# Fused HGRN2 attention and square-plus MLP: four output buffers, a last eviction in two column halves, one eviction placed earlier

## The chip, the cores and the metric

The kernel runs on one core of a Trainium2 chip. The time is that of one execution on the device, in microseconds, and the lower the better. The kernel before takes 192.82 us, the median of five runs (192.39 to 195.28). The profile is that of one further execution.

Five engines work side by side, each through its own list of instructions in order: TensorE (PE, matrix products into PSUM), VectorE (DVE), ScalarE (ACT), GpSimd (POOL) and SyncE (SP), which here only starts DMA transfers. ScalarE and GpSimd start some transfers too. An instruction that waits for a semaphore holds up everything behind it on its engine.

## What is computed

A gated linear recurrence over 768 steps for 4 x 8 heads of size 48, then a two-layer MLP on all 3072 tokens:

```python
f = 1.0 / (1.0 + np.exp(-f_logit))
for t in range(S):
    state = f[:, :, t, :, None] * state + np.einsum('bhd,bhe->bhde', k[:, :, t], v[:, :, t])
    y[:, :, t] = np.einsum('bhd,bhde->bhe', q[:, :, t], state)
...
x = attn_out.transpose(0, 2, 1, 3).reshape(B * S, H * D)    # 3072 x 384
h = x @ w_in                                                # 3072 x 2048
g = 0.5 * (h + np.sqrt(h * h + 4.0))
out = g @ w_out                                             # 3072 x 384
```

## The kernel before

The tokens are cut into 12 pairs of two blocks, 256 tokens a pair (p = 0 to 11), 128 a block. Each pair goes through the recurrence in its chunked form (small matrix products, line 424 to line 511) and then through the MLP. What follows is the MLP part, since the change touches its end alone.

- `m1.p.m` (line 551, m = 0 to 7): six matmuls that make 256 columns of h for the pair, in one PSUM bank.
- `sq.p.m` (line 560) and `rt.p.r` (line 566) on ScalarE: the square, and the square root for two m at once. `gt.p.m` (line 576) on VectorE: 0.5 h + r into the tile `g`.
- `m2.p.cn` (line 588): four matmuls each. For block c of the pair (c = 0 or 1) n runs from 0 to 3; after n = 3 one PSUM bank holds 128 tokens x 384 columns of the output. So `m2.10.03` is the last of pair 10's block 0.
- `ev.p.c` (line 595): the eviction, a copy of that bank into half c of the pair's tile `os` (128 x 2 x 384, fp32, line 597), on ScalarE (the copy of line 138) or VectorE (line 140). Tiles of the name `os` go round through `DEPTH['os']` buffers (line 29), by p modulo the depth. A copy into a buffer waits until the stores that read it before have landed.
- `st.p.cs.i` (line 605): a store to memory. i picks the partitions 0 to 63 or 64 to 127. For pairs 0 to 10 a store takes both blocks (`st10.01.0` and `st10.01.1`, 192 KB each), so it needs both evictions. For pair 11 each block has its own two stores, 96 KB each (`SPLIT_OUT`, line 26).

There is no scheduler at run time or build time: the string `ORDER` (lines 32 to 106) lists all pieces by name, with the engine behind the colon (S SyncE, A ScalarE, D VectorE, P GpSimd, T TensorE) and the PSUM banks behind the @. Lines 695 to 703 emit the pieces in this order, so it is each engine's program order. The waits are put in by the framework from what each instruction reads and writes. The list ends so:

```
gt11.2:D m2.10.03:T m1.11.4:T@4 gt11.3:D m2.11.10:T@2 sq11.4:A m2.11.00:T@0 ev9.1:A rt11.2:A m2.11.11:T st9.01.1:S st8.01.1:S
m2.10.12:T gt11.5:D st9.01.0:S m2.11.01:T gt11.4:D m2.10.13:T m2.11.02:T ev10.1:A m2.11.03:T ev10.0:A st10.01.0:S m2.11.12:T
ev11.0:D st10.01.1:S m2.11.13:T st11.0.0:A st11.0.1:S ev11.1:A st11.1.1:A st11.1.0:S
```

Read for ScalarE alone the end is: `ev9.1`, `rt11.2`, `ev10.1`, `ev10.0`, issue of `st11.0.0`, `ev11.1`, issue of `st11.1.1`. For SyncE: `st9.01.1`, `st8.01.1`, `st9.01.0`, `st10.01.0`, `st10.01.1`, `st11.0.1`, `st11.1.0`. VectorE ends with `gt11.5`, `gt11.4`, `ev11.0`.

Of the kernel before, what the change touches and what calls it, by code (L numbers as in the profile page):

```python
# [8 lines left out]
FP32 = mybir.dt.float32  # L9
FP16 = mybir.dt.float16  # L10
# [15 lines left out]
SPLIT_OUT = [11]  # L26
NHL = 2
NQK = 3
DEPTH = {'f': 3, 'q': 3, 'k': 3, 'v': 3, 'UT': 3, 's': 2, 'ep': 2, 'ea': 2, 'v16': 4, 'ge': 3, 'gs': 4, 'gb': 3, 'qkT0': 2, 'qkT1': 2, 'pm00': 2, 'pm01': 2, 'pm10': 2, 'pm11': 2, 'st0': 1, 'pc': 4, 'st1': 1, 'sn0': 2, 'sn1': 2, 'y16': 2, 'xT': 5, 'hsq': 3, 'r16': 3, 'g': 4, 'os': 2}
VDMA = []  # L30

ORDER = """
lf0.0:S lf0.1:S lq0.0:S lk0.0:S lq0.1:S TABLE:e ex0.0:A lf1.0:S ut0.0:D ex0.1:A tt0.0:D lk0.1:S ut0.1:D hi0.0:A ln0.0:A
# [66 lines left out]
m1.11.7:T@4 gt9.7:D st8.01.0:S m1.11.6:T@6 rt10.2:A m1.11.0:T@5 sq11.1:A gt10.4:D m2.9.03:T sq11.0:A m2.10.00:T@7 ev9.0:D  # L100
rt11.0:A m1.11.3:T@0 gt10.5:D m2.9.10:T@3 sq11.6:A gt11.1:D m2.10.10:T@1 sq11.3:A gt11.0:D m2.9.11:T sq11.7:A m1.11.2:T@2
m1.11.5:T@5 sq11.2:A m2.10.01:T sq11.5:A m2.10.02:T rt11.3:A m2.10.11:T rt11.1:A gt11.6:D m2.9.12:T gt11.7:D m2.9.13:T
gt11.2:D m2.10.03:T m1.11.4:T@4 gt11.3:D m2.11.10:T@2 sq11.4:A m2.11.00:T@0 ev9.1:A rt11.2:A m2.11.11:T st9.01.1:S st8.01.1:S
m2.10.12:T gt11.5:D st9.01.0:S m2.11.01:T gt11.4:D m2.10.13:T m2.11.02:T ev10.1:A m2.11.03:T ev10.0:A st10.01.0:S m2.11.12:T
ev11.0:D st10.01.1:S m2.11.13:T st11.0.0:A st11.0.1:S ev11.1:A st11.1.1:A st11.1.0:S
"""

ENGINES = {"D": "vector", "P": "gpsimd", "A": "scalar", "S": "sync", "T": "tensor"}
# [19 lines left out]
def describe(nc, W, ctx_tiles, aps):  # L128
    q, k, v, f_logit, moe_w_in, moe_w_out, out = aps
    T, sb, ps, K = ctx_tiles  # L130
    NP, H, D, NJ, NN, DM = 12, 8, 48, 3, 16, 384
# [4 lines left out]
    def copy(e, o, i):  # L136
        if e == "A":
            nc.scalar.copy(out=o, in_=i)  # L138
        else:
            eng(e).tensor_copy(out=o, in_=i)  # L140
# [3 lines left out]

    src = {"f": f_logit, "q": q, "k": k, "v": v}

    for i in range(4):
        def win(e, b, i=i):
            nc.gpsimd.dma_start(out=K["win"][i], in_=moe_w_in[:, i * 512:(i + 1) * 512].rearrange("(j p) n -> p j n", p=128))
        W.add(f"wi{i}", "P", win, makes=[f"win{i}"], dma=("w", 2.37), cost={"P": 0.83})  # L150

    for i in range(4):
        def wout(e, b, i=i):
# [3 lines left out]
    for p in range(NP):  # L157
        parts = [(0, 4), (4, 8)] if p in FINE else [(0, 8)]
        xs = range(len(parts))
        n = 384 // len(parts)  # L160
        b, c0 = divmod(p * 2, 6)
# [5 lines left out]
        for x, (h0, h1) in enumerate(parts):  # L167
            hs = slice(h0, h1)
            nh = h1 - h0
            for s in ("fqk" if p in VDMA else "fqkv"):  # L170
                def load(e, bk, s=s, x=x, hs=hs, p=p):
                    if (s, p) not in T:
# [5 lines left out]
                      dma=("l", 1.55 * nh / 8), cost={"S": 0.6})  # L178

            def ex(e, bk, x=x, hs=hs, p=p):  # L180
# [3 lines left out]
                  cost={"A": 0.2 + 0.84e-3 * 2 * n})  # L184

            last = x == len(parts) - 1
            if p in SPLIT:
                def ln(e, bk, x=x, hs=hs, p=p):
                    nc.scalar.activation(out=K["l32"][:, :, hs, 0:D], in_=T["f", p][:, hs].rearrange("p h i d -> p i h d"), func=AF.Ln, bias=1.0)
                W.add(f"ln{p}.{x}", "A", ln, reads=[f"e{p}.{x}"], makes=[f"s{p}.{x}"], uses=[("f", p), ("l32", p)], table="e",  # L190
                      cost={"A": 0.2 + 0.85e-3 * 2 * n})

                def cu(e, bk, x=x, hs=hs, h0=h0, h1=h1, p=p, last=last):
# [8 lines left out]
                    if last:  # L202
# [5 lines left out]
                      uses=[("l32", p)], banks=[f"cx{p}", f"c1{p}"], mode="F", cost={"T": 2.8 * nh / 8 + (1.0 if last else 0.0)})  # L208

                for i in range(2):  # L210
                    for nm, sgn, slot in (("ea", -1.0, 2 * i), ("ep", 1.0, 1 + 2 * i)):
                        def xp(e, bk, i=i, sgn=sgn, slot=slot, hs=hs, h0=h0, h1=h1, p=p):
                            if ("UT", p) not in T:
# [4 lines left out]
                              uses=[("UT", p), ("bank", f"c{'x1'[i]}{p}")], table="e", cost={"A": 0.17 + 0.85e-3 * n})  # L218

                for s, nm, en in ((0, "q", "ea"), (1, "k", "ep")):  # L220
                    for i in range(2):
                        def qm(e, bk, s=s, i=i, nm=nm, hs=hs, h0=h0, h1=h1, p=p):
# [3 lines left out]
                              uses=[(nm, p), ("UT", p), ("qk", p)], lock=True, cost={"D": 0.14 + 1.1e-3 * n, "P": 0.1 + 2.3e-3 * n})  # L226

            else:
# [14 lines left out]
                def ln(e, bk, x=x, hs=hs, p=p):  # L243
# [3 lines left out]
                    if ("s", p) not in T:  # L247
# [3 lines left out]
                      cost={"A": 0.2 + 0.85e-3 * n})  # L251

                if p not in DIRECT:
                    direct = p in HI_ACT

                    def hi(e, bk, x=x, hs=hs, p=p, direct=direct):
# [3 lines left out]
                        else:  # L260
                            copy(e, o, T["s", p][:, hs])
                    W.add(f"hi{p}.{x}", "A" if direct else "DPA", hi, reads=[f"t{p}.{x}" if direct else f"s{p}.{x}"], makes=[f"hi{p}.{x}"],
                          uses=[("UT" if direct else "s", p), ("hl", p)], table="e" if direct else None, lock=True, cost={"D": 0.07 + 0.9e-3 * n, "P": 0.19 + 0.86e-3 * n, "A": 0.2 + 0.85e-3 * n})
# [9 lines left out]
                def cu(e, bk, x=x, hs=hs, h0=h0, h1=h1, p=p, last=last, mats=mats):  # L273
# [12 lines left out]
                    if last:  # L286
# [10 lines left out]
                      cost={"T": full * len(mats) / 2 * nh / 8 + ((0.24 if p not in DIRECT else 0.5) if last else 0.0)})  # L297

                if p in ADD1:
                    def c1(e, bk, x=x, hs=hs, h0=h0, h1=h1, p=p):  # L300
                        if ("ea", p) not in T:
# [4 lines left out]
                          uses=[("ea", p), ("s", p), ("bank", f"cx{p}")], cost={"D": 0.15 + 1.05e-3 * n})  # L306

                for m, nm, sgn in ((0, "ep", 1.0), (1, "ea", -1.0)):
# [5 lines left out]
                    if m == 1 and p in ADD1:  # L314
                        W.add(f"{nm}{p}.{x}", "A", xp, reads=[f"cumi{p}.{x}"], makes=[f"{nm}{p}.{x}"], uses=[(nm, p)], table="e",
                              cost={"A": 0.2 + 0.85e-3 * n})
                    else:
                        W.add(f"{nm}{p}.{x}", "A", xp, reads=[f"cum{p}.{x}"], makes=[f"{nm}{p}.{x}"],
                              uses=[(nm, p), ("bank", f"c{'x1'[m]}{p}")], table="e", cost={"A": 0.17 + 0.85e-3 * n})
# [13 lines left out]
                for s, nm, en in ((0, "q", "ea"), (1, "k", "ep")):  # L333
                    def qm(e, bk, s=s, nm=nm, en=en, x=x, hs=hs, h0=h0, h1=h1, p=p):
                        for i in range(2):
# [3 lines left out]
                          uses=[(nm, p), (en, p), ("qk", p)], lock=True, cost={"D": 0.18 + 1.15e-3 * 2 * n, "P": 0.2 + 2.3e-3 * 2 * n})  # L339
# [20 lines left out]
        def ge(e, bk, p=p):  # L360
# [3 lines left out]
              cost={"A": 0.18})  # L364
# [14 lines left out]
        for cc in range(2):  # L379
            if p in XBAR:  # L380
                def tx(e, bk, cc=cc, p=p):
# [4 lines left out]
                      dma=("x", 1.9), cost={"S": 1.25})  # L386
        if p not in XBAR:
            for x, (h0, h1) in enumerate(parts):
# [15 lines left out]
                for cc in range(2):  # L404
                    def te(e, bk, x=x, j0=j0, j1=j1, cc=cc, p=p):
                        if ("qkT", p, cc) not in T:
# [3 lines left out]
                    m = (j1 - j0) * 256  # L410
                    W.add(f"te{p}.{cc}.{x}", "DA", te, reads=[f"tr{p}.{x}"], makes=[f"qkT{p}.{cc}"],
                          uses=[(f"qkT{cc}", p), ("bank", f"t{'AB'[cc]}{p}")], cost={"D": 0.15 + 0.53e-3 * m, "A": 0.17 + 0.83e-3 * m})

        both = [f"qkT{p}.0", f"qkT{p}.1"]
        for i in range(2):
# [12 lines left out]
            for h in range(2):  # L428
                key = f"{p}.{i}{h}"
                if key in PMACT:  # L430
                    def pc(e, bk, i=i, h=h, p=p):
# [3 lines left out]
                          cost={"A": 0.6})  # L435

                def pm(e, bk, i=i, h=h, p=p, key=key):
# [4 lines left out]
                      uses=[(f"pm{i}{h}", p), ("pc", 4 * p + 2 * i + h) if key in PMACT else ("bank", f"s{i}{h}.{p}")],  # L442
# [101 lines left out]
                      cost={"D": 0.35, "A": 0.49})  # L544

        for m in range(8):
            def m1(e, bk, m=m, p=p):
                T["h", p, m] = ps(bk[0], [128, 2, 2, 128], FP32)
                for a in range(2):
                    for j in range(NJ):  # L550
                        nc.tensor.matmul(out=T["h", p, m][:, a], lhsT=K["win"][m // 2][:, j, m % 2 * 256 + a * 128:m % 2 * 256 + a * 128 + 128],  # L551
                                         rhs=T["xT", p][:, :, j, :], start=(j == 0), stop=(j == NJ - 1))
            W.add(f"m1.{p}.{m}", "T", m1, reads=[f"xT{p}", f"win{m // 2}"], makes=[f"h{p}.{m}"], uses=[("xT", p)],
                  banks=[f"h{m}.{p}"], mode="F", cost={"T": 0.665})
            r, a = divmod(m, 2)

            def sq(e, bk, m=m, r=r, a=a, p=p):
                if ("hsq", p, r) not in T:
                    T["hsq", p, r] = sb("hsq", 4 * p + r, [128, 2, 512], FP16)
                nc.scalar.activation(out=T["hsq", p, r][:, a], in_=T["h", p, m].rearrange("p a c t -> p (a c t)"), func=AF.Square, scale=1.0)  # L560
            W.add(f"sq{p}.{m}", "A", sq, reads=[f"h{p}.{m}"], makes=[f"hsq{p}.{r}"], uses=[("bank", f"h{m}.{p}"), ("hsq", 4 * p + r)],
                  cost={"A": 0.585})
            if a == 1:
                def rt(e, bk, r=r, p=p):
                    T["r16", p, r] = sb("r16", 4 * p + r, [128, 2, 512], FP16)
                    nc.scalar.activation(out=T["r16", p, r], in_=T["hsq", p, r], func=AF.Sqrt, scale=0.25, bias=1.0)  # L566
                W.add(f"rt{p}.{r}", "A", rt, reads=[f"hsq{p}.{r}"], makes=[f"r16{p}.{r}"], uses=[("hsq", 4 * p + r), ("r16", 4 * p + r)],
                      table="s", cost={"A": 1.065})
# [13 lines left out]
        for cc in range(2):  # L582
            for n4 in range(4):
                def m2(e, bk, cc=cc, n4=n4, p=p):
                    if n4 == 0:
                        T["o", p, cc] = ps(bk[0], [128, DM], FP32)
                    for jn in range(4 * n4, 4 * n4 + 4):
                        nc.tensor.matmul(out=T["o", p, cc], lhsT=T["g", p][:, jn, cc * 128:(cc + 1) * 128],  # L588
                                         rhs=K["wout"][jn // 4][:, jn % 4, :], start=(jn == 0), stop=(jn == NN - 1))
                W.add(f"m2.{p}.{cc}{n4}", "T", m2,  # L590
                      reads=[f"g{p}.{2 * n4}", f"g{p}.{2 * n4 + 1}", f"wout{n4}"] + ([f"o{p}.{cc}{n4 - 1}"] if n4 else []),
                      makes=[f"o{p}.{cc}{n4}"], uses=[("g", p)] + ([("bank", f"o{cc}.{p}")] if n4 else []),
                      banks=[f"o{cc}.{p}"] if n4 == 0 else [], mode="F", cost={"T": 0.66})

            def ev(e, bk, cc=cc, p=p):
                if ("os", p) not in T:
                    T["os", p] = sb("os", p, [128, 2, DM], FP32)
                copy(e, T["os", p][:, cc], T["o", p, cc])
            W.add(f"ev{p}.{cc}", "DA", ev, reads=[f"o{p}.{cc}3"], makes=[f"os{p}.{cc}"], uses=[("bank", f"o{cc}.{p}"), ("os", p)],
                  cost={"D": 0.56, "A": 0.48})  # L600

        split = [[0], [1]] if p in SPLIT_OUT else [[0, 1]]
        for cs in split:
            for i in range(2):
                def st(e, bk, cs=cs, i=i, p=p):
                    c, n = cs[0], len(cs)
                    t0 = p * 256 + c * 128
                    eng(e).dma_start(out=out[t0:t0 + 128 * n, :].rearrange("(c u i) d -> i u c d", c=n, i=2)[i],
                                     in_=T["os", p][64 * i:64 * i + 64, c:c + n])
                W.add(f"st{p}.{''.join(map(str, cs))}.{i}", "SPA" if p in SPLIT_OUT else "S", st, reads=[f"os{p}.{c}" for c in cs], makes=[],  # L610
                      uses=[("os", p)], dma=("o", 0.28 * len(cs)), cost={"S": 0.6, "P": 0.8, "A": 0.6})


# [1 line left out]
def kernel(  # L615
# [10 lines left out]
    nc = tc.nc  # L626
# [53 lines left out]
        nc.gpsimd.tensor_copy(out=mask[:, i].rearrange("p (i t) -> p i t", i=2), in_=tri2[:, 1].unsqueeze(1).broadcast_to([128, 2, 64]))  # L680
    nc.gpsimd.tensor_copy(out=mask[:, 1, 0:64], in_=tri2[:, 0])

    win = [konst.tile([128, 3, 512], FP16, name=f"win{i}") for i in range(4)]
    wout = [konst.tile([128, 4, 384], FP16, name=f"wout{i}") for i in range(4)]

    def sb(name, seq, shape, dt):
        return sbp.tile(shape, dt, name=name, tag=f"{name}_{seq % DEPTH[name]}", bufs=1)

# [45 lines left out]
```

## Time and profile before

| | |
|---|---|
| median of five runs | 192.82 us |
| the profiled execution, whole | 192.7 us |
| its span, first to last instruction | 190.7 us |
| TensorE busy | 171.6 us, 90% |
| ScalarE busy | 156.9 us, 82% |
| VectorE busy | 150.4 us, 79% |
| GpSimd busy | 111.7 us, 59% |
| copies of `os` on ScalarE | 13, 478 ns each |
| copies of `os` on VectorE | 11, 551 ns each |
| stores of `os` issued by SyncE, by ScalarE | 24, 2 |
| last matmul ends | 185.2 us |
| granted TensorE clock, mean | 0.976 |

The profiled execution is one of its own, 0.1 us under the median of the five. Its span leaves out 2.0 us that lie around the first and the last instruction. A share of busy time is a mean over the whole span: here TensorE is at nine tenths or more in nearly every slice from 68 us to 185 us, and idle or waiting for data in much of the first 68 us. What an edit at the end of the kernel is worth is read from the last few microseconds, and from the question whether anything before them waits for what it touches. All times below are us from the start of the span.

### The profile page before, as it was taken

The page shows a single profiled execution, that of the slowest core. Times are in us where ns is not written, and L with a number is a line of the kernel's source. Part 1 is how long each engine was busy: PE and PEld are TensorE (multiplying, and loading weights), DVE is VectorE, ACT ScalarE, POOL GpSimd, SP SyncE. Part 2 cuts the span into 40 slices and gives each one's busy share as a digit, 9 for nine tenths or more (in the row PEclk, how much of TensorE's full clock was granted, in tenths as well). Part 3 has the DMA queues.
Part 4 walks back from the last instruction along what each step waited for, and adds up shares of the span by engine and source line. Part 5 has one row for each costly group of instructions (what it writes and reads, how often), then busy time and mean ns, then how long its engine had stood idle before and what let it go on. Part 6 is the DMA issues. An engine that isn't in the chain of part 4 may idle for free.

```text
span 190.7 us, 5590 instructions
## 1 busy us (share of the span) xinstructions
PE 171.6 (90%) x2287; PEld 124.3 (65%) x2287; DVE 150.4 (79%) x279; ACT 156.9 (82%) x254; POOL 111.7 (59%) x139
## 2 busy tenths in 40 slices
PE   0649489999999999999999999999999999999980
PEld 0425367776677666887677786787787787776640
DVE  6789957989999998989889877888899965652420
ACT  4578877999988998989999998998999499887420
POOL 4227785999899999979948988879150000000000
PEclk9999957999999999999999999999999999999997
DMA  5999999899999998999989993992848424010056
GB/s 138 276 259 288 254 206 224 187 201 204 271 279 208 229 278 213 227 264 174 185 190 244 177 254 79 254 228 57 139 75 82 64 64 84 3 41 0 10 126 156
DMA packets 80505, 32.87 MB, mean 172 GB/s; under 512 B 73824, under 2 KB 80480, under 8 KB 80480
## 3 DMA queue, kind: packets, MB, share of 16 engines
q1 hardware_dynamic: 76608, 29.17, 72.5%
q0 software_dynamic: 3712, 3.15, 10.3%
q8 instruction: 18, 0.29, 0.6%
q10 hardware_dynamic: 160, 0.20, 0.5%
q14 instruction: 7, 0.06, 0.1%
HBM read 25.17 MB, written 4.72 MB: 157 GB/s over the span
## 4 chain that ended last, share of the span: by engine, by line
PE 60%; DMA 16%; POOL 11%; SPq 4%; issue 2%; DVE 2%; ACT 1%; ACTq 0%; POOLq 0%; DVEq 0%
PE ps L551 26%; PE ps L588 24%; DMA k<-in_k_dram 8%; DMA win<-in_moe_w_in_dram 4%; POOL qk L143 4%; PE ps L424 3%; DMA f<-in_f_logit_dram 3%; SPq L175 3%; PE ps L502 2%; POOL k L143 2%; PE ps L452 2%; PE ps L511 2%; DMA out_dram<-os 1%; POOL hl L267 1%; POOL v L140 1%
## 5 line engine op out<-in xcount | busy, mean ns | idle before, releaser
L551 PE MATMUL ps<-xT,win 128*128 128x256 f16 x576 | 73.2, 278 | 2.6 <-DMA win<-in_moe_w_in_dram 2.5
L576 DVE SCALAR_TENSOR_TENSOR g<-ps,r 128x512 f16<-128x512 f32 x96 | 62.3, 683 | 15.9 <-ACT r L566 15.8
L588 PE MATMUL ps<-wout,g 128*128 128x384 f16 x384 | 71.3, 326 | 0.3 <-DMA wout<-in_moe_w_out_dram 0.3
L551 PEld LDWEIGHTS <-win 128*128 128x128 f16 x576 | 55.6, 99 | 13.1 <-DMA win<-in_moe_w_in_dram 3.1
L560 ACT ACTIVATE hsq<-ps 128x512 f16<-128x512 f32 x96 | 53.6, 593 | 12.4 <-PE ps L551 12.0
L566 ACT ACTIVATE r<-hsq 128x1024 f16<-128x1024 f16 x48 | 50.7, 1058 | 1.9 <-DVE g L576 0.7
L588 PEld LDWEIGHTS <-g 128*128 128x128 f16 x384 | 36.1, 98 | 19.9 <-issue 0.6
L439 DVE TENSOR_TENSOR pm<-ps,mask 128x512 f16<-128x512 f32 x48 | 30.9, 683 | 5.7 <-PE ps L424 5.4
L143 POOL TENSOR_TENSOR qk<-q,ea 128x384 f16<-128x384 f32 x20 | 19.6, 1000 | 2.6 <-ACT ea L313 1.3
L143 POOL TENSOR_TENSOR qk<-k,ep 128x384 f16<-128x384 f32 x20 | 19.7, 1010 | 0.1
L143 POOL TENSOR_TENSOR k<-k,UT 128x768 f32<-128x768 f32 x8 | 14.5, 1815 | 1.8 <-DMA k<-in_k_dram 1.8
L143 POOL TENSOR_TENSOR UT<-UT 128x384 f32<-128x384 f32 (+1 forms) x9 | 9.2, 1020 | 10.7 <-DVE UT L232 10.7
L284 PE MATMUL ps<-hl,tri 128*128 128x384 f16 (+1 forms) x34 | 9.0, 375 | 6.3 <-ACT hl L259 5.3
L182 ACT ACTIVATE f<-f 128x768 f32<-128x768 f32 (+1 forms) x13 | 10.2, 794 | 4.6 <-DMA f<-in_f_logit_dram 4.5
L424 PE MATMUL ps<-qkT 48*64 48x128 f16 x384 | 9.6, 235 | 2.0 <-ACT qkT L138 1.5
L140 DVE CAST y<-ps 128x384 f16<-128x384 f32 x16 | 8.8, 552 | 2.8 <-PE ps L511 2.7
L424 PEld LDWEIGHTS <-qkT 48*64 48x64 f16 x384 | 6.6, 115 | 6.5 <-issue 3.7
L138 ACT COPY os<-ps 128x384 f32<-128x384 f32 x13 | 6.1, 478 | 5.3 <-DMA out_dram<-os 2.9
L267 POOL TENSOR_TENSOR hl<-s,hl 128x384 f16<-128x384 f32 (+1 forms) x11 | 9.7, 882 | 1.1 <-ACT s L249 0.7
L140 POOL CAST v<-v 128x768 f16<-128x768 f32 x11 | 9.1, 827 | 1.6 <-DMA v<-in_v_dram 1.6
L143 POOL TENSOR_TENSOR q<-q,UT 128x384 f32<-128x384 f32 x8 | 8.0, 997 | 2.9 <-DMA q<-in_q_dram 2.9
L232 DVE TENSOR_SCALAR UT<-f 128x768 f32<-128x768 f32 (+1 forms) x13 | 8.4, 644 | 1.0 <-ACT f L182 1.0
(72 smaller groups left out, 184.2 us busy)
## 6 DMA issues: line engine op xcount, KB each, us to landing
f<-in_f_logit_dram SPq DMA_DIRECT2D x11, 384.0 KB, 5.6
k<-in_k_dram SPq DMA_DIRECT2D x11, 384.0 KB, 5.5
q<-in_q_dram SPq DMA_DIRECT2D x11, 384.0 KB, 5.4
v<-in_v_dram SPq DMA_DIRECT2D x11, 384.0 KB, 4.6
out_dram<-os SPq DMA_DIRECT2D x22, 192.0 KB, 3.4
win<-in_moe_w_in_dram POOLq DMA_DIRECT2D x4, 384.0 KB, 9.0
wout<-in_moe_w_out_dram POOLq DMA_DIRECT2D x4, 384.0 KB, 8.8
f<-in_f_logit_dram SPq DMA_DIRECT2D x2, 192.0 KB, 2.9
```

The source lines that it names most:

```text
L140: eng(e).tensor_copy(out=o, in_=i)
L143: eng(e).tensor_tensor(out=o, in0=a, in1=b, op=ALU.mult)
L182: nc.scalar.activation(out=t, in_=t, func=AF.Exp, scale=-1.0)
L267: eng(e).tensor_tensor(out=hl[:, 1, hs, 0:D], in0=T["s", p][:, hs], in1=hl[:, 0, hs, 0:D], op=ALU.subtract)
L284: nc.tensor.matmul(out=T["cum", p, m][:, h0 * D:h1 * D], lhsT=tri[:, m], rhs=t[:, hs, 0:D], start=(r == 0), stop=(r == len(terms) - 1), sk ...
L424: nc.tensor.matmul(out=T["sc", p, i, h][64 * cc:64 * cc + 64, j, :], lhsT=t[r, 1, j, i, :], rhs=t[r, 0, j], start=True, stop=True)
L439: eng(e).tensor_tensor(out=T["pm", p, i, h], in0=T["pc", p, i, h] if key in PMACT else T["sc", p, i, h], in1=K["mask"][:, i].unsqueeze(1). ...
L551: nc.tensor.matmul(out=T["h", p, m][:, a], lhsT=K["win"][m // 2][:, j, m % 2 * 256 + a * 128:m % 2 * 256 + a * 128 + 128], rhs=T["xT", p][ ...
L560: nc.scalar.activation(out=T["hsq", p, r][:, a], in_=T["h", p, m].rearrange("p a c t -> p (a c t)"), func=AF.Square, scale=1.0)
L566: nc.scalar.activation(out=T["r16", p, r], in_=T["hsq", p, r], func=AF.Sqrt, scale=0.25, bias=1.0)
L576: nc.vector.scalar_tensor_tensor(out=T["g", p][:, 2 * m:2 * m + 2, :].rearrange("p a t -> p (a t)"), in0=T["h", p, m].rearrange("p a c t - ...
L588: nc.tensor.matmul(out=T["o", p, cc], lhsT=T["g", p][:, jn, cc * 128:(cc + 1) * 128], rhs=K["wout"][jn // 4][:, jn % 4, :], start=(jn == 0 ...
```

## The change

Three things change, and two that only rewrite code.

- `os` has four buffers instead of two.
- `ev10.0` (the eviction of block 0 of pair 10, which is block 20 of 24) moves from behind `ev10.1` to right behind `rt11.2` in the order.
- `ev11.1` becomes `ev11.1a`, columns 0 to 191 on ScalarE, and `ev11.1b`, columns 192 to 383 on VectorE. Both stores of that block read both halves.
- The slices of `w_in` are written as a list `WI` with the same bounds as before, and the engines that the planner's description allows for a store are another set (`OUT_ACT`). The order gives every store the engine that it had.

```diff
-DEPTH = {... 'g': 4, 'os': 2}
+DEPTH = {... 'g': 4, 'os': 4}
+WI = [(0, 512), (512, 1024), (1024, 1536), (1536, 2048)]
+OUT_ACT = [9, 10, 11]
...
-gt11.2:D m2.10.03:T m1.11.4:T@4 gt11.3:D m2.11.10:T@2 sq11.4:A m2.11.00:T@0 ev9.1:A rt11.2:A m2.11.11:T st9.01.1:S st8.01.1:S
-m2.10.12:T gt11.5:D st9.01.0:S m2.11.01:T gt11.4:D m2.10.13:T m2.11.02:T ev10.1:A m2.11.03:T ev10.0:A st10.01.0:S m2.11.12:T
-ev11.0:D st10.01.1:S m2.11.13:T st11.0.0:A st11.0.1:S ev11.1:A st11.1.1:A st11.1.0:S
+gt11.2:D m2.10.03:T m1.11.4:T@4 gt11.3:D m2.11.10:T@2 sq11.4:A m2.11.00:T@0 ev9.1:A rt11.2:A ev10.0:A m2.11.11:T st9.01.1:S
+st8.01.1:S m2.10.12:T gt11.5:D st9.01.0:S m2.11.01:T gt11.4:D m2.10.13:T m2.11.02:T ev10.1:A m2.11.03:T st10.01.0:S m2.11.12:T
+ev11.0:D st10.01.1:S m2.11.13:T st11.0.0:A st11.0.1:S ev11.1a:A ev11.1b:D st11.1.1:A st11.1.0:S
...
+            cuts = [(0, 192), (192, 384)] if p == NP - 1 and cc == 1 else [(0, 384)]
+            for z, (d0, d1) in enumerate(cuts):
+                def ev(e, bk, cc=cc, p=p, d0=d0, d1=d1):
...
-                copy(e, T["os", p][:, cc], T["o", p, cc])
+                    copy(e, T["os", p][:, cc, d0:d1], T["o", p, cc][:, d0:d1])
...
-                W.add(f"st{p}.{''.join(map(str, cs))}.{i}", "SPA" if p in SPLIT_OUT else "S", st, reads=[f"os{p}.{c}" for c in cs], makes=[],
+                W.add(f"st{p}.{''.join(map(str, cs))}.{i}", "SA" if p in OUT_ACT else "S", st,
+                      reads=[r for c in cs for r in ([f"os{p}.{c}a", f"os{p}.{c}b"] if p == NP - 1 and c == 1 else [f"os{p}.{c}"])], makes=[],
```

More of the change, by code (lines that the diff above doesn't have):

```diff
@@ L28 @@
 NQK = 3
-DEPTH = {'f': 3, 'q': 3, 'k': 3, 'v': 3, 'UT': 3, 's': 2, 'ep': 2, 'ea': 2, 'v16': 4, 'ge': 3, 'gs': 4, 'gb': 3, 'qkT0': 2, 'qkT1': 2, 'pm00': 2, 'pm01': 2, 'pm10': 2, 'pm11': 2, 'st0': 1, 'pc': 4, 'st1': 1, 'sn0': 2, 'sn1': 2, 'y16': 2, 'xT': 5, 'hsq': 3, 'r16': 3, 'g': 4, 'os': 2}
+DEPTH = {'f': 3, 'q': 3, 'k': 3, 'v': 3, 'UT': 3, 's': 2, 'ep': 2, 'ea': 2, 'v16': 4, 'ge': 3, 'gs': 4, 'gb': 3, 'qkT0': 2, 'qkT1': 2, 'pm00': 2, 'pm01': 2, 'pm10': 2, 'pm11': 2, 'st0': 1, 'pc': 4, 'st1': 1, 'sn0': 2, 'sn1': 2, 'y16': 2, 'xT': 5, 'hsq': 3, 'r16': 3, 'g': 4, 'os': 4}
 VDMA = []
+WI = [(0, 512), (512, 1024), (1024, 1536), (1536, 2048)]
+OUT_ACT = [9, 10, 11]
 ORDER = """
@@ L145, in describe, with win @@
     src = {"f": f_logit, "q": q, "k": k, "v": v}
[L147 to L150, printed above, removed]
+    for i, (n0, n1) in enumerate(WI):
+        def win(e, b, i=i, n0=n0, n1=n1):
+            nc.gpsimd.dma_start(out=K["win"][i], in_=moe_w_in[:, n0:n1].rearrange("(j p) n -> p j n", p=128))
+        W.add(f"wi{i}", "P", win, makes=[f"win{i}"], dma=("w", 2.37 * (n1 - n0) / 512 + 0.2 * (n1 - n0 < 512)), cost={"P": 0.83})
     for i in range(4):
@@ L546, in describe, with m1 @@
         for m in range(8):
-            def m1(e, bk, m=m, p=p):
+            wp = max(i for i, (n0, n1) in enumerate(WI) if n0 <= m * 256)
+            wc = m * 256 - WI[wp][0]
+            def m1(e, bk, m=m, p=p, wp=wp, wc=wc):
                 T["h", p, m] = ps(bk[0], [128, 2, 2, 128], FP32)
@@ L550, in m1 @@
                     for j in range(NJ):
-                        nc.tensor.matmul(out=T["h", p, m][:, a], lhsT=K["win"][m // 2][:, j, m % 2 * 256 + a * 128:m % 2 * 256 + a * 128 + 128],
+                        nc.tensor.matmul(out=T["h", p, m][:, a], lhsT=K["win"][wp][:, j, wc + a * 128:wc + a * 128 + 128],
                                          rhs=T["xT", p][:, :, j, :], start=(j == 0), stop=(j == NJ - 1))
-            W.add(f"m1.{p}.{m}", "T", m1, reads=[f"xT{p}", f"win{m // 2}"], makes=[f"h{p}.{m}"], uses=[("xT", p)],
+            W.add(f"m1.{p}.{m}", "T", m1, reads=[f"xT{p}", f"win{wp}"], makes=[f"h{p}.{m}"], uses=[("xT", p)],
                   banks=[f"h{m}.{p}"], mode="F", cost={"T": 0.665})
@@ L593, in describe @@
                       banks=[f"o{cc}.{p}"] if n4 == 0 else [], mode="F", cost={"T": 0.66})
-            def ev(e, bk, cc=cc, p=p):
-                if ("os", p) not in T:
-                    T["os", p] = sb("os", p, [128, 2, DM], FP32)
-                copy(e, T["os", p][:, cc], T["o", p, cc])
-            W.add(f"ev{p}.{cc}", "DA", ev, reads=[f"o{p}.{cc}3"], makes=[f"os{p}.{cc}"], uses=[("bank", f"o{cc}.{p}"), ("os", p)],
-                  cost={"D": 0.56, "A": 0.48})
+            cuts = [(0, 192), (192, 384)] if p == NP - 1 and cc == 1 else [(0, 384)]
+            for z, (d0, d1) in enumerate(cuts):
+                def ev(e, bk, cc=cc, p=p, d0=d0, d1=d1):
+                    if ("os", p) not in T:
+                        T["os", p] = sb("os", p, [128, 2, DM], FP32)
+                    copy(e, T["os", p][:, cc, d0:d1], T["o", p, cc][:, d0:d1])
+                W.add(f"ev{p}.{cc}{'ab'[z] if len(cuts) > 1 else ''}", "DA", ev, reads=[f"o{p}.{cc}3"], makes=[f"os{p}.{cc}{'ab'[z] if len(cuts) > 1 else ''}"],
+                      uses=[("bank", f"o{cc}.{p}"), ("os", p)], cost={"D": 0.14 + 1.1e-3 * (d1 - d0), "A": 0.1 + 1e-3 * (d1 - d0)})
         split = [[0], [1]] if p in SPLIT_OUT else [[0, 1]]
@@ L681 @@
     nc.gpsimd.tensor_copy(out=mask[:, 1, 0:64], in_=tri2[:, 0])
-    win = [konst.tile([128, 3, 512], FP16, name=f"win{i}") for i in range(4)]
+    win = [konst.tile([128, 3, n1 - n0], FP16, name=f"win{i}") for i, (n0, n1) in enumerate(WI)]
     wout = [konst.tile([128, 4, 384], FP16, name=f"wout{i}") for i in range(4)]
```

## The prediction

> **What bounds the kernel now.** I read the page's busy times first (TensorE 90% of the span), then the 40 slices (TensorE is at nine tenths from slice 14 to slice 38), then the chain of waits. From about 68 us the chain is TensorE without a gap, and from 178.8 us it runs over evictions and stores instead. So an edit to output buffers and evictions can pay in two places: where a wait on an output buffer holds an engine that TensorE needs, or in the tail behind the last matmul. The view of the tile `os` says which. It lists what the evictions waited for in the whole run:
>
> ```profile
> its engine sat idle before it (us, times) until:
>   DMA out_dram<-os: 5.0, 2
>   PE ps L588: 3.5, 8
> ```
>
> Of 24 evictions just two waited for an earlier store to land. The timeline of ScalarE and of VectorE from 178 us on (start us, duration us, engine, line, operation, count, idle time before it and its releaser) shows that both lie in the tail:
>
> ```profile
> 178.76 0.60 ACT L560 ACTIVATE hsq<-ps 128x512 f16<-128x512 f32 x1 [2.07 <-PE ps L551]
> ...
> 183.58 0.86 ACT L138 COPY os<-ps 128x384 f32<-128x384 f32 x2 [2.90 <-DMA out_dram<-os]
> 184.74 0.55 ACTq L608 DMA_DIRECT2D out_dram<-os  x1
> 185.46 0.48 ACT L138 COPY os<-ps 128x384 f32<-128x384 f32 x1 [1.01 <-PE ps L588]
> 185.97 0.48 ACTq L608 DMA_DIRECT2D out_dram<-os  x1
> ...
> 184.14 0.56 DVE L140 COPY os<-ps 128x384 f32<-128x384 f32 x1 [2.14 <-DMA out_dram<-os]
> ```
>
> The two copies at 183.58 are `ev10.1` and `ev10.0`; 184.14 is `ev11.0`; 185.46 is `ev11.1`, behind the last matmul, which ends at 185.22. A 'q' row is a store being issued, not work. Only TensorE works beside them, until 185.22. But the last eviction does not set the end. The four last stores on SyncE's queue, each looked at alone, do:
>
> ```profile
> 184.47 0.59 SPq L608 DMA_DIRECT2D out_dram<-os  x1
> 185.11 0.61 SPq L608 DMA_DIRECT2D out_dram<-os  x1
> 185.81 0.81 SPq L608 DMA_DIRECT2D out_dram<-os  x1
> 186.71 0.98 SPq L608 DMA_DIRECT2D out_dram<-os  x1
> ```
>
> They are `st10.01.0`, `st10.01.1`, `st11.0.1`, `st11.1.0`. The first starts when the pair of ScalarE copies ends (183.58 + 0.86 = 184.44), and from there SyncE issues without a pause: `ev11.1` is done at 185.94, yet its store is issued only at 186.71, 0.77 us later, because SyncE is still busy with the others. The list of DMA issues gives the time from issue to landing: five of the tail's 192 KB stores, and then that last store alone:
>
> ```profile
> out_dram<-os SPq DMA_DIRECT2D x5, 192.0 KB, 2.8
> ...
> out_dram<-os SPq DMA_DIRECT2D x1, 96.0 KB, 2.9
> ```
>
> So the last landing is 186.71 + 2.9 = 189.6, and 1.05 us of closing barrier makes 190.7. The table by stretches (us, then busy time of each engine, granted clock, DMA share, GB/s) tells whether bytes or issues set that:
>
> ```profile
> 184.40:185.70 1.30, 0.82 (x6) 0.29 (x3) 0.30 (x1) 0.29 (x2) 0.00 (x0) 1.00 0.00 0
> 185.70:187.00 1.30, 0.00 (x0) 0.00 (x0) 0.00 (x0) 0.23 (x1) 0.00 (x0) 1.00 0.90 191
> 187.00:188.00 1.00, 0.00 (x0) 0.00 (x0) 0.00 (x0) 0.00 (x0) 0.00 (x0) 1.00 0.96 275
> 188.00:189.30 1.30, 0.00 (x0) 0.00 (x0) 0.00 (x0) 0.00 (x0) 0.00 (x0) 0.64 0.74 202
> ```
>
> After the issue at 184.47 nothing moves until 185.7, about 1.25 us; then 191 x 1.3 + 275 + 202 x 1.3 = 786 KB leave in 3.6 us, 218 GB/s, with the engines nearly full. The tail is thus a train whose start (`ev10.1`) and whose last wagon (`st11.1.0`) are both late.
>
> **Four buffers.** Pair 10 takes the buffer that pair 6 left, pair 11 that of pair 7; those stores were issued before 160 us. The two buffer waits go, and what is late next is TensorE. Its matmuls of line 588 run without a gap from 178.56 to 185.22 in blocks of four, 0.65 us each (page: x384, 326 ns each, overlapped). Counted back in the order list, `m2.10.13` ends at 185.22 - 4 x 0.65 = 182.62 and `m2.11.03` at 185.22 - 2 x 0.65 = 183.92. ScalarE starts about 0.04 us after a matmul ends (178.72 to 178.76 in the row above). So `ev10.1` runs 182.66 to 183.14 (0.48 us) instead of from 183.58, and `ev11.0` on VectorE 183.96 to 184.52 (0.56 us) instead of from 184.14, which is only 0.18 us earlier. Before the tail no eviction waited on a store, so there the buffers are worth nothing; and TensorE, which covers them, has no wait on a copy of `os` in the list of waits.
>
> **`ev10.0` moved forward** (the eviction of block 20, pair 10, half 0). It goes ahead of `ev10.1` on ScalarE, right behind `rt11.2`, which ends at 180.68. Its matmuls stand before `m1.11.4` in TensorE's order, hence ended before 177.90. It runs 180.7 to 181.2, in idle time; `ev10.1`, queued behind it, starts 1.5 us later. It issues no DMA and passes no queue of SyncE or GpSimd: the stores keep their order. Its worth: `st10` needs both halves, so without the move it would start 0.38 us later (in the pair above the second copy ends that much after the first).
>
> **SyncE then.** `st10.01.0` 183.16 to 183.75, `st10.01.1` 183.80 to 184.41; `st11.0.1` waits for `ev11.0` and runs 184.55 to 185.36 (at 0.81). SyncE is free 0.6 us before the last eviction ends. On ScalarE `st11.0.0` is released at the same moment: 184.55 to 185.10. The buffer checks that stood between it and the last eviction (185.28 to 185.46) take until 185.2 at most, so ScalarE is ready for the last matmul: first half at 185.26, not 185.46.
>
> **The last eviction in halves.** This is where a rule weighs against the change. Rows: a 128x192 read of PSUM on ScalarE took 318 and 331 ns (the exponentials of line 313), so 0.325. On VectorE 384 columns take 551 ns and 512 take 683, 1.03 ns a column, so 192 columns cost 551 - 198 = 0.353. If both engines read at once, the eviction is over at 185.26 + 0.35 = 185.61. But both halves lie in one PSUM bank, and the Trainium skill (PSUM — Partial Sum Buffer, Terms) says that two engines must not touch the same bank and partitions at once, two reads included. No row of this trace has two engines in one bank. In the changed kernel's instruction list the VectorE half waits for ScalarE's semaphore, value and all that of the ScalarE half: the rule is obeyed, and the halves run one after the other. Then: 185.26 + 0.325 + 0.03 + 0.353 = 185.96. I take that: it is what is built. The split costs 0.22 us against one copy from 185.26 (185.74), and cancels the earlier start: the last stores can go at 185.99, against 185.97 on ScalarE before.
>
> **Sum.** `st11.1.0` starts at 185.99 instead of 186.71. Bytes: the train starts at 183.16 + 1.25 = 184.4, and 3.6 us of bytes end at 188.0, so it is the issue that decides. Issue to landing, not shown for this mix: 2.7 at the least (the shortest in the run), 3.3 at the most (ScalarE's own last store, which had to share with the `st10` stores; these now go earlier). I take 2.8, the median of the tail's stores, as the queue ahead of it is shorter than before. Landing 188.79 instead of 189.64: **0.85 us less** (0.95 to 0.35 for 2.7 and 3.3). Span 189.8, its run 192.7 - 0.85 = 191.85. The profiled run lies 0.1 under the median of 192.82; I say 191.9.
>
> **Nothing else moves.** The rewritten slices of the input weight, and the list of engines allowed for stores, give the same instructions; TensorE's and GpSimd's lists are unchanged.
>
> **Rivals.**
> 1. *Hidden anyway.* The last two stores now leave both queues in the same moment, so ScalarE's may land last, with its 3.3 us, or the issue of `st11.0.0` takes 0.98 as SyncE's last one did, and pushes the last eviction 0.4 us. For it: six stores share the 16 engines, at 0.9 busy. Against: the bytes would be done at 188.0. Landing 189.25, gain 0.35 to 0.45: 192.3 to 192.4, no difference to be told.
> 2. *Slower: issues in pairs get in each other's way.* `st11.0.0` with `st11.0.1`, then `st11.1.1` with `st11.1.0`, are each released by one semaphore on two queues. If a common issue takes f times as long, the last eviction is late by 0.55(f-1) and the last store by a further 0.98(f-1), 1.53(f-1) together. It eats the 0.85 at f = 1.55, and is 0.3% slower from f = 1.93; at f = 2 the time is 193.4. For it: the issue rows of these stores go from 595 to 2111 ns in the run. Against: ScalarE's issue at 185.97 lay wholly inside SyncE's at 185.81 and took 0.48, the shortest of all.
> 3. *More than forecast.* With landing at 2.7 or a last issue of 0.6 instead of 0.98, the gain is 0.95 to 1.3: 191.4 to 191.8. For it: the issue rows were longer with more stores queued. Against: two stores still stand ahead.
>
> **How the numbers follow.** Forecast 0.55, rival 1 0.22, rival 2 0.06, rival 3 0.17. A measurement of this kernel tells about 0.3% (0.58 us) from no change. The forecast (its own band 191.7 to 192.1) and rival 3 are faster by more than that, 0.72 in all; rival 1 is the same, 0.22; rival 2 slower, 0.06. The range 191.4 to 192.5 takes in rivals 1 and 3 and leaves out rival 2 and the scatter of runs.
>
> **What would show it.** Right: the copies of `os` at 182.66, 183.96 and 185.26 with TensorE as the releaser; the VectorE half right behind the ScalarE half; SyncE's four issues at 183.2, 183.8, 184.55, 186.0; the last landing near 188.8. Wrong: both halves at once (then 0.35 us more), a copy that still waits for a store, an issue over 1 us, ScalarE's store landing last, or a difference before 178 us, which nothing here explains.

## The result, and the profile after

The changed kernel takes 191.2 us, the median of 44 runs (189.87 to 193.21), against 192.5 us of the kernel before in 79 runs (190.88 to 196.1). The ratio is 0.9943, 95% interval 0.9928 to 0.9958; it leaves out the runs more than 1.5% above the fastest of their kernel, a slower state that both kernels have, and so is not quite the quotient of the two medians. That is 1.1 us less (0.8 to 1.4): faster, as forecast, and the 0.85 us of the forecast lies within the interval. The forecast's range of 191.4 to 192.5 us was counted from 192.82 us, the median of five runs. The ratio makes 191.7 us of that; the 191.2 itself lies just below the range, because the kernel before also came out lower in 79 runs than in five. The profiled run took 192.04 us, its span is 190.13.

Read against each other, the two profiles seem to say less: the spans differ by only 0.55 us. The reason lies ahead of the tail: the last matmul ends at 185.22 us in the profile before and at 185.84 after, 0.62 us later. That end moves from run to run in both kernels (shown below). So this document measures the **tail**: the end of the span less the end of the last matmul, both taken from the trace. It was 190.69 - 185.22 = 5.47 us and is 190.13 - 185.84 = 4.29 us, 1.18 less, which lies within the interval of the ratio.

The view of the tile `os` in the changed kernel (us in total, times) no longer has a store in its list of waits:

```profile
its engine sat idle before it (us, times) until:
  PE ps L593: 8.1, 10
  ACT os L140: 1.1, 1
```

The timelines of ScalarE and VectorE at the end (start, duration, engine, line, operation, count, idle time before it and its releaser) show the copies one by one:

```profile
181.19 0.48 ACT L140 COPY os<-ps 128x384 f32<-128x384 f32 x1
183.28 0.48 ACT L140 COPY os<-ps 128x384 f32<-128x384 f32 x1 [1.61 <-PE ps L593]
185.17 0.55 ACTq L615 DMA_DIRECT2D out_dram<-os  x1
185.88 0.32 ACT L140 COPY os<-ps 128x192 f32<-128x192 f32 x1 [2.12 <-PE ps L593]
186.62 0.51 ACTq L615 DMA_DIRECT2D out_dram<-os  x1
...
184.58 0.56 DVE L142 COPY os<-ps 128x384 f32<-128x384 f32 x1 [1.96 <-PE ps L593]
186.23 0.36 DVE L142 COPY os<-ps 128x192 f32<-128x192 f32 x1 [1.09 <-ACT os L140]
```

`ev10.0` runs early, in idle time; `ev10.1`, `ev11.0` and the first half of the last eviction start when TensorE lets them. The VectorE half has ScalarE as its releaser: it starts at 186.23, after the ScalarE half has ended at 186.20. The halves run one after the other.

SyncE's last four stores, each looked at alone:

```profile
183.78 0.59 SPq L615 DMA_DIRECT2D out_dram<-os  x1
184.42 0.61 SPq L615 DMA_DIRECT2D out_dram<-os  x1
185.16 0.51 SPq L615 DMA_DIRECT2D out_dram<-os  x1
186.62 0.49 SPq L615 DMA_DIRECT2D out_dram<-os  x1
```

Between the third, which ends at 185.67, and the fourth SyncE is idle for 0.95 us; before there was no gap. And the last two took less time to issue than before (0.51 and 0.49 against 0.81 and 0.98). The list of DMA issues gives the time from issue to landing of the two last stores:

```profile
out_dram<-os SPq DMA_DIRECT2D x1, 96.0 KB, 2.2
out_dram<-os ACTq DMA_DIRECT2D x1, 96.0 KB, 2.4
```

So the last landing is ScalarE's, at 186.62 + 2.43 = 189.05. After the last matmul that is 3.20 us, and was 4.42.

### The profile page after: what moved, and what is told of

Read it like the earlier page. It is cut to its first block, busy times and chain, and to the rows that moved or that the text cites. A ratio compares the mean times of both kernels' runs of the same rounds, so it can differ in the third digit from the quotient of the medians.

```text
span 190.1 us, 5584 instructions
## 1 busy us (share of the span) xinstructions
PE 171.0 (90%) x2287; PEld 124.5 (66%) x2287; DVE 149.8 (79%) x280; ACT 156.6 (82%) x254; POOL 111.2 (58%) x139
## 3 DMA queue, kind: packets, MB, share of 16 engines
HBM read 25.17 MB, written 4.72 MB: 157 GB/s over the span
## 4 chain that ended last, share of the span: by engine, by line
PE 81%; DMA 11%; SPq 3%; POOL 1%; ACT 1%; DVE 1%; issue 0%
PE ps L593 33%; PE ps L556 33%; DMA win<-in_moe_w_in_dram 5%; SPq L177 3%; PE ps L426 3%; PE ps L504 3%; DMA q<-in_q_dram 3%; DMA f<-in_f_logit_dram 3%; PE ps L454 3%; PE ps L513 2%; PE ps L286 2%; PE ps L292 1%; PE ps L464 1%; PE ps L537 1%; POOL q L145 1%
## 5 line engine op out<-in xcount | busy, mean ns | idle before, releaser
L556 PE MATMUL ps<-xT,win 128*128 128x256 f16 x576 | 72.4, 276 | 4.4 <-DMA win<-in_moe_w_in_dram 4.3
L269 POOL TENSOR_TENSOR hl<-s,hl 128x384 f16<-128x384 f32 (+1 forms) x11 | 10.3, 933 | 1.5 <-ACT s L251 0.7
L140 ACT COPY os<-ps 128x384 f32<-128x384 f32 (+1 forms) x13 | 6.0, 464 | 5.1 <-PE ps L593 5.1
L142 DVE COPY os<-ps 128x384 f32<-128x384 f32 (+1 forms) x12 | 6.4, 535 | 4.3 <-PE ps L593 3.1
```

The lines of the kernel that those rows point to most:

```text
L269: eng(e).tensor_tensor(out=hl[:, 1, hs, 0:D], in0=T["s", p][:, hs], in1=hl[:, 0, hs, 0:D], op=ALU.subtract)
L556: nc.tensor.matmul(out=T["h", p, m][:, a], lhsT=K["win"][wp][:, j, wc + a * 128:wc + a * 128 + 128], rhs=T["xT", p][:, :, j, :], start=(j ...
```

## The experiments

Every run was profiled, and each is read by its tail, since the time of a single execution moves by more than any of these parts is worth. "Issued" is when the last store's issue starts, "landed" when the last store's data has landed, both counted from the end of the last matmul, in us. A run for which no ratio is given is a single execution. The edits are shown against the kernel before for "buffers alone" and against the changed kernel for all others; what is left out of a line is marked by three dots.

| kernel | buffers | move | halves | issued | landed | tail |
|---|---|---|---|---|---|---|
| before | 2 | no | no | 1.49 | 4.42 | 5.47 |
| before, again | 2 | no | no | 1.59 | 4.69 | 5.73 |
| move alone | 2 | yes | no | 1.53 | 4.43 | 5.47 |
| halves alone | 2 | no | yes | 1.60 | 4.72 | 5.76 |
| buffers alone | 4 | no | no | 0.55 | 3.37 | 4.48 |
| buffers and halves | 4 | no | yes | 0.78 | 3.20 | 4.30 |
| buffers and move | 4 | yes | no | 0.55 | 3.07 | 4.17 |
| after (the change) | 4 | yes | yes | 0.78 | 3.20 | 4.29 |
| after, again | 4 | yes | yes | 0.78 | 3.21 | 4.31 |
| after, three buffers | 3 | yes | yes | 0.78 | 3.19 | 4.29 |
| pair 10 first | 4 | yes | no | 0.55 | 2.94 | 4.05 |

**Buffers alone.**

```diff
-... 'g': 4, 'os': 2}
+... 'g': 4, 'os': 4}
```

> Kernel before with four buffers; no move, last eviction whole. Measure: the tail, from the end of the last matmul to the end of the span (5.47 us before, 4.29 after the change). Theory (buffers free the eviction of block 21, SyncE's queue is empty when the last eviction ends, and from then on only issue and landing count): st10 goes 0.38 us later than with the move, but SyncE is still free in time, and one whole copy is 0.25 us shorter than two halves in a row; tail 4.0 to 4.1. Rival 1 (the move is what brings it): tail 5.1 to 5.5. Rival 2 (bytes ahead in the queue set the end): 4.3 to 4.5.

Tail 4.48; ratio 0.9934 (0.9897 to 0.9972). Of the 1.18 us between the two first profiles, 0.99 come with this one digit. The timeline of ScalarE in this run, for the copies of pair 10 and the last copy:

```profile
181.13 0.86 ACT L138 COPY os<-ps 128x384 f32<-128x384 f32 x2 [1.98 <-PE ps L588]
...
183.73 0.48 ACT L138 COPY os<-ps 128x384 f32<-128x384 f32 x1 [1.74 <-PE ps L588]
```

Both are released by TensorE, whose last matmul ends at 183.69 here. The mechanism is as expected, the number is not: 4.0 to 4.1 was wrong, and the rival that lets bytes in the queue count (4.3 to 4.5) has it. The last stores were issued at 0.54 and 0.55, with both `st10` stores still on their way (they land at 1.11 and 1.85), and took 2.66 (SyncE) and 2.83 us (ScalarE) to land.

**Buffers and move, last eviction whole.**

```diff
-... ev11.1a:A ev11.1b:D st11.1.1:A st11.1.0:S
+... ev11.1:A st11.1.1:A st11.1.0:S
```

> Four buffers and the move, last eviction whole on ScalarE. Theory: last stores are issued about 0.25 us sooner after the last matmul than with halves (0.52 instead of 0.77 us), tail 4.0 to 4.1, time 0.1% under the changed kernel. Rival (the split helps, as its two engines suggest): tail 4.5. Rival (bytes set the end): 4.3, as after.

Tail 4.17; ratio 0.9935 (0.9891 to 0.9979). The whole copy gets the last stores away 0.23 us sooner than the halves, and the end comes 0.12 us sooner. With the move in place the halves cost, but half of the delay is hidden. The tail lies between the theory (4.0 to 4.1) and the rivals (4.3 and 4.5).

**Three buffers.**

```diff
-... 'g': 4, 'os': 4}
+... 'g': 4, 'os': 3}
```

> The changed kernel with three buffers. Pair 11 then takes pair 8's buffer, whose stores land about 0.4 us before the matmuls of block 22 end, and pair 10 that of pair 7. Theory: no eviction waits for a store, tail 4.25 to 4.35 as after. Rival (the fourth buffer counts): block 22's eviction waits for a store, tail longer by 0.1 us or more.

Tail 4.29, as with four; ratio 0.9944 (0.9905 to 0.9983). The fourth buffer does nothing here.

**The change once more.** No edit.

> The changed kernel once more, as the measure for the other three. Theory: tail 4.25 to 4.35, while the time of the last matmul (185.2 before, 185.8 after in the two profiles) moves by some tenths of a microsecond either way from run to run. Rival (the buffers move something early and cost 0.6 us there): last matmul at 185.8 again here and in the runs with four buffers, and at 185.2 in runs with two.

Tail 4.31; ratio 0.9933 (0.9899 to 0.9967). Last matmul at 184.94, not at 185.8 again as the rival had it.

**The move alone.** Two buffers, `ev10.0` behind `rt11.2`, last eviction whole.

> The move alone: two buffers, last eviction whole. The moved copy has to wait for the stores of pair 8, as both copies of pair 10 did before. Theory: no gain, tail 5.4 to 5.5 as before. Rival (the move has a worth of its own): 5.0 to 5.2.

Tail 5.47, the same as in the first profile before. The kernel before had 5.73 in a second profile (below), so single profiles with two buffers can't show a gain of less than about 0.3 us; the rival's 5.0 to 5.2 did not come. With two buffers both copies of pair 10 wait for the stores of pair 8. The run's timeline of ScalarE shows them side by side again, where the moved one should stand alone:

```profile
183.76 0.86 ACT L140 COPY os<-ps 128x384 f32<-128x384 f32 x2 [2.94 <-DMA out_dram<-os]
```

**The halves alone.** Two buffers, order of before, `ev11.1a` and `ev11.1b`.

> The split alone: two buffers, order of before. Theory: SyncE is still busy with its queue when the last eviction ends, so a later end of that eviction is mostly hidden on SyncE; tail 5.4 to 5.6. Rival (the split shortens the tail): under 5.3.

Tail 5.76. That is over the expected 5.4 to 5.6. The kernel before has 5.47 and 5.73 (below), so this shows no gain, and whether the halves cost anything here is not shown.

**The kernel before once more.** No edit.

> The kernel before once more. Theory: tail 5.4 to 5.5 again, while the last matmul ends anywhere between 183.5 and 186 us; that spread is the front of the kernel and belongs to no part of the change. Rival (the kernel before has a front of its own, at 185.2): 185.0 to 185.4 and the changed kernels elsewhere.

Tail 5.73, not 5.4 to 5.5: with two buffers it is not as constant as thought. Everything from the copies of pair 10 on came later by 0.04 to 0.27 us against the last matmul. Against this profile the change gains 1.44 us of tail, and the buffers alone 1.25. Last matmul at 183.41, so the front is scatter: over all runs it ends from 183.41 (two buffers) to 187.80 (four buffers), with both kinds mixed in between. In the first pair of profiles, most of it is a wait for the input weight. This is the row of the line that uses that weight, of the page before, in its last columns: idle time, and what ended it.

```profile
L551 PE MATMUL ps<-xT,win 128*128 128x256 f16 x576 | 73.2, 278 | 2.6 <-DMA win<-in_moe_w_in_dram 2.5
```

And of the page after:

```profile
L556 PE MATMUL ps<-xT,win 128*128 128x256 f16 x576 | 72.4, 276 | 4.4 <-DMA win<-in_moe_w_in_dram 4.3
```

The waits for these loads are 1.8 us longer after the change, though it touches none of them; part of it is made up before the middle of the kernel. An effect of the buffers on the front is not excluded by single profiles, but the ratio leaves no room for one of that size.

**Buffers and halves, no move.**

```diff
-... ev9.1:A rt11.2:A ev10.0:A m2.11.11:T ...
+... ev9.1:A rt11.2:A m2.11.11:T ...
-... m2.11.03:T st10.01.0:S ...
+... m2.11.03:T ev10.0:A st10.01.0:S ...
```

> Four buffers and the split, without the move: the fourth corner beside four buffers alone (tail 4.48), with the move (4.17), with move and split (4.29). Theory: the last stores are issued 0.24 us later than with a whole copy, but the st10 stores ahead of them, late by 0.38 without the move, cover part of that; tail 4.5 to 4.6. Rival (the costs add in full): 4.7 or more.

Tail 4.30: the expectation of 4.5 to 4.6 was wrong. With halves the move is worth nothing (4.30 without, 4.29 with); with a whole copy it is worth 0.31 (4.48 without, 4.17 with). And without the move, the halves, which send the last stores off 0.23 us later, end 0.18 us sooner than the whole copy. A later issue that lands earlier is odd. The DMA packets in the two traces tell where it happens: the last packet with data ends 2.85 us after the last matmul without the halves and 2.84 with them, so the earlier issue moved no byte to an earlier end; the last landing follows about 0.5 us behind that packet in the one run and about 0.35 in the other. What draws out this last part is open, and each of the two corners is a single profile.

**Pair 10 first.** A version that might beat both: `m2.10.12` and `m2.10.13` go before `m2.11.10`, so that pair 10 is out of the way early, and `ev10.1` follows right behind `ev10.0`. Everything else as with buffers and move.

```diff
-... gt11.3:D m2.11.10:T@2 sq11.4:A m2.11.00:T@0 ev9.1:A rt11.2:A ev10.0:A m2.11.11:T ...
+... gt11.3:D m2.10.12:T m2.10.13:T m2.11.10:T@2 sq11.4:A m2.11.00:T@0 ev9.1:A rt11.2:A ev10.0:A ev10.1:A m2.11.11:T ...
-... m2.10.12:T gt11.5:D st9.01.0:S m2.11.01:T gt11.4:D m2.10.13:T m2.11.02:T ev10.1:A m2.11.03:T ...
+... gt11.5:D st9.01.0:S m2.11.01:T gt11.4:D m2.11.02:T m2.11.03:T ...
```

> Four buffers, the move, last eviction whole, and m2.10.12 and m2.10.13 placed before m2.11.10 on TensorE, so that pair 10 is complete 5.2 us before the last matmul ends instead of 2.6. Question: does the queue ahead of the last two stores (393 KB of st10) still cost time when those are issued at once after the last eviction? In the run with four buffers and the move the last store was issued at 0.54 after the last matmul and landed 2.5 later, tail 4.17. Theory (bytes ahead still count for some tenths): st10 has landed by 0.2 after the last matmul, the last stores land 2.2 after their issue, tail 3.80 to 3.95, TensorE not delayed. Rival (issue and fixed latency alone): tail stays 4.1 to 4.2.

Tail 4.05, the shortest; ratio to before 0.9931 (0.9900 to 0.9963). The `st10` stores had landed at 0.37 after the last matmul, and yet this gains only 0.12 us over buffers and move. The tail lies between the two expectations: the `st10` bytes ahead cost about a tenth of a microsecond, and the rest, 2.16 us on SyncE and 2.40 on ScalarE, is what a 96 KB store takes with only block 22's pair of 96 KB stores ahead of it. In this run's view of `os` one copy, the last, is put down to a store (3.8 us). It starts 0.04 us after the last matmul, as in all runs with four buffers, and pair 7's stores, the only ones on its buffer, were issued more than 20 us earlier: TensorE released it. By tail it beats the changed kernel by 0.24 us. By time the two can't be told apart.

The last three runs start from this kernel and take that remaining time apart.

**The last pair in stores of 192 KB.**

```diff
-SPLIT_OUT = [11]
+SPLIT_OUT = []
-... st11.0.0:A st11.0.1:S ev11.1:A st11.1.1:A st11.1.0:S
+... ev11.1:A st11.01.1:A st11.01.0:S
```

> As the run with pair 10 first, but pair 11 goes out in two stores of 192 KB, one on each queue, after its last eviction, in place of four of 96 KB. Issue to landing of the last store was 2.2 us (SyncE) and 2.4 us (ScalarE) there. Theory (the size of the last stores sets the time from issue to landing; the 2.8 of the prediction was a figure for 192 KB): 2.8 to 3.3 us on both, tail 4.4 to 4.9. Rival (a fixed latency, whatever the size): tail 4.0 to 4.15.

Issue to landing, from the list of DMA issues of this run:

```profile
out_dram<-os SPq DMA_DIRECT2D x1, 192.0 KB, 2.8
out_dram<-os ACTq DMA_DIRECT2D x1, 192.0 KB, 3.3
```

Both were issued at 0.54 after the last matmul, when the `st10` stores had landed (0.40). Twice the bytes on both queues, 0.68 us (SyncE) and 0.92 (ScalarE) more: the size counts, and a fixed latency is excluded. The tail, 5.09, is above the expected 4.9; 0.13 of it is a longer end of the kernel, 1.23 us from the last landing to the end of the span instead of 1.10.

**Both last stores on SyncE.**

```diff
-... st11.1.1:A st11.1.0:S
+... st11.1.1:S st11.1.0:S
```

> As the run with pair 10 first, but both last stores are issued by SyncE, one after the other. Theory (two queues save one issue, about 0.5 us, and nothing else): the second is issued 0.55 us later, the last landing 0.3 us later (ScalarE's landed 0.24 after SyncE's before), tail 4.3 to 4.4. Rival (one queue is no slower, since the transfers share the same DMA engines anyway): 4.0 to 4.15.

Tail 4.31, as the theory had it: issues at 0.54 and 1.08, landings at 2.64 and 3.27.

**The last two stores changed over.**

```diff
-... st11.1.1:A st11.1.0:S
+... st11.1.0:A st11.1.1:S
```

> As the run with pair 10 first, with the two last stores changed over: ScalarE issues the one of partitions 0 to 63, SyncE that of 64 to 127. In all runs with four buffers ScalarE's store landed 0.13 to 0.24 us after SyncE's though both were issued within 0.01 us. Theory (it belongs to the queue, which is served second): ScalarE's is the later one again. Rival (it belongs to the partitions or rows): SyncE's is now the later one. Tail 4.0 to 4.1 in both.

```profile
out_dram<-os SPq DMA_DIRECT2D x1, 96.0 KB, 2.2
out_dram<-os ACTq DMA_DIRECT2D x1, 96.0 KB, 2.4
```

These are the last stores in this run's list of issues. Tail 4.05. ScalarE's is again the later one, with the other rows: it belongs to the queue, or to the engine that issues it.

## Why the prediction was right, and what it mis-sized

- **The bound.** Right. What counted was a train of stores behind a buffer wait. Buffers alone bring 0.99 us of the 1.18, and take away both waits on stores. In the middle of the kernel nothing shows: from the 145th to the last matmul with the input weight it is 108.91 us before and 108.92 after.
- **The times of the copies.** Counted from the last matmul's end, the prediction had `ev10.1` at -2.56, `ev11.0` at -1.26 and the first half at 0.04; the profile has these same three numbers. SyncE's four issues also come at the forecast places, within 0.01 us.
- **The last eviction in halves.** The two durations were forecast as 0.325 and 0.353 and are 0.318 and 0.357. The halves are serial, which keeps the rule on PSUM banks in the Trainium skill (PSUM — Partial Sum Buffer, Terms) that two engines must not touch one bank and the same partitions at once: the VectorE half waits for ScalarE's, and the last stores go off at 0.77 after the last matmul, forecast 0.77; both engines at once would have given about 0.42. No run tried that. The price of 0.22 us against one copy is there in the issue (0.23), but only 0.12 of it reaches the end, so "it is the issue that decides" was half right: the bytes in the queue count too.
- **The move.** Forecast at 0.38 us of `st10`. True of that store, but not of the end: 0.31 with a whole last copy, 0.01 in the change as it was made. These are differences between single profiles.
- **The step that was off: issue to landing of the last store.** The sum took 2.8 us, a median of stores of 192 KB with others in the queue. The last ones are of 96 KB; they took 2.19 (SyncE) and 2.43 (ScalarE). With the later one, the landing is 0.37 us earlier than forecast (3.20 against 188.79 - 185.22 = 3.57 after the last matmul), and 0.85 + 0.37 = 1.22 is the gain between the landings, 4.42 - 3.20. Both the size and the queue have a part in it: 192 KB with `st10` landed took 2.84 and 3.31, and 96 KB with `st10` still on its way took 2.66 and 2.83 (buffers alone). What the shorter issue adds, 0.49 instead of the 0.98 that SyncE's last one took before, no run separates; the 2.66 had an issue of 0.49 too.
- **The rivals.** "More than forecast" is what came: issue and landing were shorter, as it named, and the tail's gain lies within its 0.95 to 1.3. "Hidden anyway" named rightly that ScalarE's store would land last, but it does so after 2.4 us, not 3.3. "Issues in pairs get in each other's way" is refuted: the pair of stores at 185.16 took 0.51 and 0.55, the pair at 186.62 took 0.49 and 0.51. Issued together, they were no slower.
- **The signs of being wrong.** Two of those that the prediction listed came. ScalarE's store landed last; it did so in every run with three or four buffers in which the two engines issued the last two stores together, and cost 0.24 us here, less than the shorter landing brought. And a difference stood before 178 us: the scatter of the front.
- **The profile's own time.** Set against the profiled run alone, 192.7, the forecast of 191.85 looks poor beside the second profile's 192.04. That is the front, 0.62 us in the other direction, which no reading of the change could give.

One thing the forecast did not follow: it took the late buffers as given. The chain of waits of the profile before (start, duration, what) shows why they were late:

```profile
179.25 0.48 ACT os L138
179.73 0.02 issue
179.75 0.59 SPq L608
180.34 0.05 issue
180.40 0.88 SPq L608
181.28 0.05 issue
181.33 2.69 DMA out_dram<-os
```

These are `ev9.1`, the issues of `st9.01.1` and `st8.01.1`, and `st9.01.0` up to its landing, which releases `ev11.0`. `st8.01.1` holds the buffer that `ev10.1` waits for: it lands at 183.48, and `ev10.1` starts at 183.58. Pair 8 had been evicted long before: its last copy is this row, and its other store, `st8.01.0`, was issued at 166.43.

```profile
165.82 0.55 DVE L140 COPY os<-ps 128x384 f32<-128x384 f32 x1
```

`st8.01.1` was 14 us late because in SyncE's list it stands behind `st9.01.1`, which waits for `ev9.1`. An estimate from these rows: right behind `st8.01.0` it would have landed by about 170, and `st9.01.0`, issued at 180.40 instead of 181.33, would have landed at 183.1 to 183.5 (2.7 to 3.1 us, as these stores took), before TensorE lets `ev11.0` go at 183.96. Moving that one store might have removed both waits with two buffers. No run tried it.

## What to carry to other kernels

At the end of a kernel, look at the store queue from the last store backwards, for the first store of the train that waits. Here it waits for a copy that waits for a buffer. More buffers are worth the time by which that copy comes sooner, 0.92 us for `ev10.1`, and not the whole idle time of 2.9 us in front of it. Then ask what kept the buffer: here a store that stood late in its engine's list.

Splitting the last eviction over two engines made it longer here, as the halves in one PSUM bank ran one after the other. With the move it cost 0.12 us of tail, without the move the tail was 0.18 shorter with it, a single profile each. Halves in two banks were not tried. The shortest tail had one whole copy and 96 KB stores, one on each of two queues. And compare short tails by their distance from the last matmul, in more than one profile of each kernel, not by whole times that scatter more than the change is worth.

## What the runs showed of the hardware

- The issue of a 96 KB store on SyncE took 0.49 to 0.59 us in the runs with three or four buffers, and 0.72 to 0.98 in those with two. The number of stores on their way does not explain it: with the same two stores on SyncE's queue and one on ScalarE's, the issue of `st11.0.1` took 0.81 before and 0.55 with buffers alone. The cause is open.
- Stores of 96 KB issued within 0.01 us on SyncE's and on ScalarE's queue, the last two of the kernel, land 0.17 to 0.25 us apart in eight runs, ScalarE's later, whichever half of the partitions it carries (2.71 and 2.95 after the last matmul in the run with the two changed over, 2.70 and 2.94 in the run with pair 10 first). For 192 KB it was 0.48.
- From issue to landing, a store took 2.16 us for 96 KB (pair 10 first) and 2.84 for 192 KB (last pair in stores of 192 KB) on SyncE, with a store of the same size on ScalarE's queue each time. Doubling the bytes added 0.68 us; if the first 96 KB cost as much, which is an estimate, about a third of the 2.16 goes with the bytes.
